# Four one-bank PSUM tiles, a pair-wise plain eviction and a split attention copy in a linear-attention and two-FFN kernel

## The chip, the cores and the metric

The kernel runs on one core of one Trainium2 chip. The metric is the device time of one execution in microseconds (us), as the median of several runs. Engines are named as the profile names them: PE (TensorE matmul), PEld (its weight load), DVE (VectorE), ACT (ScalarE), POOL (GpSimd) and SP (SyncE, which issues all DMAs here).

## The reference

Everything is in fp32. Linear attention over 8 batches, 8 heads, 576 positions and head width 64 feeds an RMS norm over the head width; the result, seen as 4608 tokens of 512 channels, goes through two feed-forward networks of width 2048.

```python
kv = np.einsum('bhsd,bhse->bhde', k, v)
out = np.einsum('bhsd,bhde->bhse', q, kv)
rms = np.sqrt(np.mean(out * out, axis=-1, keepdims=True) + 1e-06)
x = (out / rms * g_norm).transpose(0, 2, 1, 3).reshape(B * S, H * D)
h = x @ w_in;  g = np.maximum(h, 0) + alpha * np.minimum(h, 0);  x = g @ w_out      # layer 0
h = x @ w_in2; g = h / (1 + np.exp(-1.702 * h));                 y = g @ w_out2     # layer 1
```

## The kernel before

**Blocks and the two ways of multiplying.** The 4608 tokens are nine blocks j of 512. An fp32 product is made of three fp32r matmuls of 128x512 (high by high, high by low, low by high). Blocks 0, 1 and 2 of layer 0 and block 0 of layer 1 are done in plain form (`gemm_in` into a bank named h, `gemm_out` into four banks named y, one for each chunk c of 128 rows, summed over 16 steps m). All other blocks are done two at a time by a seven-product scheme (`pair_in`, `pair_out`): a step is one product, six matmuls. In-steps go into banks named X or Z, out-steps into two-bank tiles named V or W. The in-steps of two values of k (call them k0 and k1) alternate: product p for k0, product p for k1, next product for k0, and so on. X holds products 1, 6, 7, 4 on top of each other, Z product 2, and then 5 and 3; after each product the bank is read (ACT, L1166, 128x512 copy; DVE, L1158 and L1156, 128x512 add) before the next product is added in it. A run's out-steps start 26 in-steps after its in-steps (`LAGP`); from there in-steps and out-steps alternate.

**Where the order comes from.** The program first notes its operations with an engine, a cost and what each reads and writes. `arrange` plays them through a small model of the engines and gives each a start and a place in memory. `emit` does that `PASSES` times with other weights (random numbers from `SEED`), keeps the pass with the earliest end and writes all operations out in the order of their starts. So every engine's queue is fixed before the run; the tile framework puts in the semaphore waits, from the order in which instructions are written out and from the tiles that they touch.

**PSUM.** Eight banks of 512 words per partition. `SLOTS` cuts them in four slots of two banks: one of class h (plain h, Z, the first block's transposed x), two of class y (the plain y, V, W), one of class a (kv sums, transposed q, attention output ops, later blocks' transposed x, X). `at_place` opens one framework tile for a whole slot and hands out slices of it, as long as any part of the slot is in use:

```python
SLOTS += [(UNITS + 2 * i, 2, c) for i, c in enumerate("hyya")]
...
        opened[s] = (stay, kind, pool.tile([P, size * UNIT], kind, tag=f"s{s}", name=name))
    _, kind, t = opened[s]
    t = t[:, (u - u0) * UNIT : (u - u0 + n) * UNIT]
```

Thus a slot's two banks carry one tile name: a transposed q can appear as "kvps", the first plain h as "xTps".

**Attention (`job_out`).** For later blocks the output of two pairs of heads takes both a banks at once ("aa"), and one ACT copy of 128x1024 (L608) moves it to SBUF. **Weights.** In the first 200 us the 16 weight tiles of layer 0 are unpacked on ACT, DVE and POOL and split by DVE into their low part (L698 and L700, tile w). **The end of a plain block.** Each of the four chunks y is copied by an instruction of its own, even chunks on ACT and odd ones on DVE, and stored by one DMA.

Of the kernel before, what the change touches and what calls it, by code (L numbers as in the profile page):

```python
# [10 lines left out]
F32 = mybir.dt.float32  # L11
# [4 lines left out]
AF = mybir.ActivationFunctionType  # L16
# [3 lines left out]
P = 128  # L20
TB = 512
# [28 lines left out]
MM, TR, ACT, DVE, POOL, ISSUE, LAND, RATE, HOP = 0.227, 0.109, 0.63, 0.67, 1.27, 0.55, 2.2, 0.335, 0.2  # L50
ACT2, DVE2, POOL2 = 1.06, 1.17, 2.35
# [8 lines left out]
BACKLOG = 2.0  # L60
URGENT = 10.0
LD_LOW = {"4": 10}
PASSES = 30
SEED = 1
GAP, SLOW = 1.8, 3.4

RINGS = (3, 2, 2, 6)
# [11 lines left out]
def linear_attention_two_ffn_kernel(  # L79
# [25 lines left out]
    nc = tc.nc  # L105
# [43 lines left out]
    ops = []  # L149
# [57 lines left out]
    def tl(key):  # L207
        return tiles[key]
# [346 lines left out]
    def job_out(j, pp):  # L555

        heads = (2 * pp, 2 * pp + 1)
        bank, sq, xn = ((what, j, pp) for what in ("ops", "sq", "xn"))
        small = {}
        parts = [(t, *run) for t in range(NT4) for run in runs((NT4 * j + t) * P, P)]  # L560
        batches = sorted({b for _, _, _, b, _ in parts})

        def fn():
            for t, off, n, b, s in parts:
                for i, p in enumerate(heads):
                    nc.tensor.matmul(
                        tl(bank)[off : off + n, i, t],
                        lhsT=tl(("qT", j, p))[:, t * P + off : t * P + off + n],
                        rhs=tl(("kvb", b % 2))[:, p, :],
                        start=True,  # L570
                        stop=True,
                    )

        held = ("oc", j, pp) if j else bank

        def o3(key=held):
            t = tl(key)
            return t if key == ("oc", j, pp) else t.rearrange("p i t (e d) -> p (i t e) d", d=D)
# [22 lines left out]
        note(  # L601
            "PE", 0.46 * len(parts), fn,
            reads=[x for p in heads for x in ((("qT", j, p), 0), held_by["qT", j, p])] + [(("kvb", b % 2), p) for b in batches for p in heads],
            writes=[(bank, 0)], new=[(bank, [P, 2, NT4, P], F32, "aa" if j else "yy")], aside=True,
        )
        if j:
# [4 lines left out]
        note(  # L611
            "ACT", ACT2, lambda: nc.scalar.activation(out=tl(sq), in_=o3(), func=AF.Square), reads=[(held, 0)],
            writes=[(sq, 0)], new=[(sq, [P, 2 * G, D], F32, "4")],
        )
        note("DVE", 1.4, mean, reads=[(sq, 0)], writes=[(("sa", j, pp), 0)])
        note("ACT", 0.21, root, reads=[(("sa", j, pp), 0)], writes=[(("sr", j, pp), 0)])
        note(
            "DVE", 1.9, scale, reads=[(held, 0), (("sr", j, pp), 0), (("sa", j, pp), 0)], writes=[(xn, 0)],
            new=[(xn, [P, 2 * G, D], F32, "4")],
        )  # L620

# [342 lines left out]
    def gemm_out(l, j, m, m0, m1):  # L964

        if l == 0:
            weight1("wo", m)
        else:
            weight2("wo", m)
        (w, w_keys), gs = w_key(l, "wo", m), ("gs", l, j, m)  # L970
        for c in range(4):
            y = ("y", l, j, m0, c)
            sl = slice(c * P, (c + 1) * P)

            def fn(y=y, sl=sl, c=c):
                gh, gl = tl(gs)[:, 0], tl(gs)[:, 1]
                if l == 0:
                    wt = w()[:, c // 2, :, c % 2 * P : (c % 2 + 1) * P]
                    trip = ((wt[:, 0], gh), (wt[:, 0], gl), (wt[:, 1], gh))
                else:  # L980
                    wh, wl = w()[:, :, 0], w()[:, :, 1]
                    trip = ((gh[:, sl], wh), (gh[:, sl], wl), (gl[:, sl], wh))
                mm3(tl(y), trip, m == m0, m == m1)

            note(
                "PE", 3 * MM, fn, reads=[*w_keys, (gs, 0), (gs, 1)], writes=[(y, 0)],
                new=[(y, [P, TB], F32, "y")] if m == m0 else [],
            )
        if m < m1:
            return  # L990
        for c in range(4):
            y, ev, part = ("y", l, j, m0, c), ("ev", l, j, m0, c), ("part", l, j, c)
            new = [(ev, [P, TB], F32, "2")]
            if m0 > 0:
                note(
                    "SP", ISSUE, lambda part=part, c=c: nc.sync.dma_start(out=tl(part), in_=yp[c]),
                    reads=[(("yp", c), 0)], writes=[(part, 0)], new=[(part, [P, TB], F32, "2")], ahead=20.0,
                    slack=None, mb=0.26,
                )
                note(  # L1000
                    "DVE", DVE,
                    lambda y=y, ev=ev, part=part: nc.vector.tensor_tensor(
                        out=tl(ev), in0=tl(y), in1=tl(part), op=ALU.add
                    ),
                    reads=[(y, 0), (part, 0)], writes=[(ev, 0)], new=new, slack=2.0,
                )
            else:
                copy = nc.vector.tensor_copy if c % 2 else nc.scalar.copy

                def evict(y=y, ev=ev, copy=copy):  # L1010
                    if l == 0:
                        copy(tl(ev), tl(y))
                        return
                    for h in range(2):
                        sl = slice(h * HB, (h + 1) * HB)
                        copy(
                            tl(ev)[:, sl].rearrange("p (i c f) -> p i c f", c=2, f=32),
                            tl(y)[:, sl].rearrange("p (c i f) -> p i c f", c=2, f=32),
                        )

                note(
                    "DVE" if c % 2 else "ACT", DVE if c % 2 else ACT, evict, reads=[(y, 0)], writes=[(ev, 0)], new=new,
                    slack=2.0,
                )
            if l:
                dst, key = out[j * TB + c * P : j * TB + (c + 1) * P, :], ("out", j, c)
            elif m == M - 1:
                dst, key = x2d[j][c], ("dr", 1, j, c)
            else:
                dst, key = yp[c], ("yp", c)  # L1030
            note(
                "SP", ISSUE, lambda dst=dst, ev=ev: nc.sync.dma_start(out=dst, in_=tl(ev)), reads=[(ev, 0)],
                writes=[(key, 0)], mb=0.26,
            )

    def plain(steps, jobs):
# [342 lines left out]
```

## Time and profile before

| | |
|---|---|
| median of 3 runs | 1572.46 us (1572.04 to 1574.06) |
| the profiled execution | 1569.55 us, its span 1567.8 us |
| PE busy | 1520.3 us, 97% of the span, 7376 matmuls |
| DVE busy | 1150.9 us, 73% |
| ACT busy | 764.7 us, 49% |
| POOL busy | 279.6 us, 18% |
| mean granted TensorE clock | 0.994 of full speed |

The span runs from the first to the last instruction; 1.75 us of the execution lie around it. Matmuls are pipelined, and one of 128x512 shows some 390 ns though the next starts after about 227, so busy time hides short gaps: the count of matmuls in a stretch says more.

### The profile page before, as it was taken

The numbers are of one execution on the slowest core, as the hardware profiler recorded it, in microseconds if no ns is written. First come the engines' busy times: TensorE is split into PE (matmuls) and PEld (weight loads), VectorE is DVE, ScalarE is ACT, GpSimd is POOL, SyncE is SP. The second block draws the span as 40 slices with busy tenths as digits, with TensorE's granted clock in tenths as the row PEclk, the third lists the DMA queues.
The fourth block names the chain that finished last, engine by engine and source line by source line (L and its number), as shares of the span: only waits on it lengthen the run. The fifth ranks groups of instructions, "written<-read, shape, count | busy, mean of one in ns | idle before, by whom it ended". The sixth has DMA issues, their size and how long they took to land.

```text
span 1567.8 us, 19613 instructions
## 1 busy us (share of the span) xinstructions
PE 1520.3 (97%) x7376; PEld 1244.5 (79%) x7376; DVE 1150.9 (73%) x1170; ACT 764.7 (49%) x958; POOL 279.6 (18%) x186
## 2 busy tenths in 40 slices
PE   5899999999899999999999999999999999999998
PEld 4688888887687878877877888888888888888787
DVE  4999965698689998999998867664766485557511
ACT  4876544455355455544455655434544454445221
POOL 1322531275322123212420320000000000000000
PEclk8999999999999999999999999999999999999999
DMA  9899786757689789979798997576667676755963
GB/s 263 253 311 292 197 213 191 200 167 272 219 285 341 256 310 334 322 253 355 259 331 310 351 321 284 186 233 220 242 196 229 198 253 206 227 195 189 280 189 107
DMA packets 240654, 393.48 MB, mean 251 GB/s; under 512 B 94128, under 2 KB 124848, under 8 KB 240560
## 3 DMA queue, kind: packets, MB, share of 16 engines
q1 hardware_dynamic: 240560, 392.23, 77.2%
q8 instruction: 58, 0.95, 0.2%
q14 instruction: 36, 0.29, 0.1%
HBM read 302.00 MB, written 90.18 MB: 250 GB/s over the span
## 4 chain that ended last, share of the span: by engine, by line
PE 66%; DVE 2%; ACT 1%; issue 1%; DMA 0%; POOL 0%; SPq 0%; DVEq 0%; ACTq 0%; POOLq 0%
PE V L927 18%; PE X L927 17%; PE Z L927 13%; PE W L927 13%; PE h L927 3%; PE y L927 3%; ACT gr L691 0%; DVE gr L698 0%; DMA t<-x2d 0%; DVE gl L1158 0%; ACT gl L1166 0%; DVE gt L1158 0%; POOL kvb L774 0%; ACT xc L691 0%; DVE gt L891 0%
## 5 line engine op out<-in xcount | busy, mean ns | idle before, releaser
L927 PE MATMUL X<-xc,pi 128*128 128x512 f32 x912 | 233.7, 392 | 4.2 <-DVE gl L1158 3.3
L927 PEld LDWEIGHTS X<-xc,pi 128*128 128x128 f32 x912 | 169.6, 188 | 45.5 <-DVE gl L1158 7.6
L927 PE MATMUL V<-gr,x 128*128 128x512 f32 x804 | 203.9, 389 | 0.0
L927 PEld LDWEIGHTS V<-gr,x 128*128 128x128 f32 x804 | 151.0, 188 | 31.7
L927 PE MATMUL Z<-xc,pi 128*128 128x512 f32 x648 | 166.7, 393 | 2.9 <-ACT gl L1166 2.8
L927 PE MATMUL W<-gr,x 128*128 128x512 f32 x636 | 161.3, 389 | 0.0
L927 PEld LDWEIGHTS Z<-xc,pi 128*128 128x128 f32 x648 | 120.3, 188 | 33.5 <-ACT gl L1166 7.1
L927 PE MATMUL h<-x,w 128*128 128x512 f32 x576 | 142.6, 395 | 0.7 <-ACT acc L952 0.7
L927 PEld LDWEIGHTS W<-gr,x 128*128 128x128 f32 x636 | 119.4, 188 | 24.9
L927 PEld LDWEIGHTS h<-x,w 128*128 128x128 f32 x576 | 106.2, 188 | 22.6 <-ACT acc L952 1.1
L691 ACT ACTIVATE gr<-gt 128x1024 fp32r<-128x1024 f32 x84 | 88.8, 1059 | 63.1 <-DVE gt L891 24.8
L698 DVE TENSOR_TENSOR gr<-gl,gr 128x1024 fp32r<-128x1024 f32 x56 | 74.9, 1338 | 56.9 <-ACT gr L691 56.9
L927 PE MATMUL V<-gr,po 128*128 128x512 f32 x456 | 114.6, 389 | 0.0
L698 DVE TENSOR_TENSOR gr<-gt,gr 128x1024 fp32r<-128x1024 f32 x84 | 105.2, 1257 | 3.7 <-ACT gr L691 3.7
L927 PEld LDWEIGHTS V<-gr,po 128*128 128x128 f32 x456 | 85.6, 188 | 17.8
L927 PE MATMUL X<-xc,po 128*128 128x512 f32 x360 | 91.5, 389 | 1.3 <-ACT gl L1181 1.3
L858 POOL TENSOR_TENSOR da<-da 128x256 f32<-128x256 f32 x68 | 71.2, 1048 | 82.5 <-DVE wsp L698 77.9
L927 PEld LDWEIGHTS X<-xc,po 128*128 128x128 f32 x360 | 67.5, 188 | 15.6 <-ACT gl L1181 1.7
L927 PE MATMUL W<-gr,po 128*128 128x512 f32 x312 | 78.4, 389 | 0.0
L927 PE MATMUL Z<-xc,po 128*128 128x512 f32 x300 | 77.0, 392 | 0.2
L1166 ACT ACTIVATE gt<-X 128x512 f32<-128x512 f32 x64 | 38.3, 598 | 79.1 <-PE X L927 79.0
L691 ACT ACTIVATE gr<-gl 128x1024 fp32r<-128x1024 f32 x56 | 59.3, 1058 | 33.2 <-PE V L927 22.0
(507 smaller groups left out, 2698.7 us busy)
## 6 DMA issues: line engine op xcount, KB each, us to landing
po<-w1wo SPq DMA_DIRECT2D x69, 512.0 KB, 3.8
pi<-w0wi SPq DMA_DIRECT2D x68, 512.0 KB, 5.7
x<-w0wo SPq DMA_DIRECT2D x68, 512.0 KB, 5.2
pi<-w1wi SPq DMA_DIRECT2D x62, 512.0 KB, 5.0
po<-w1wi SPq DMA_DIRECT2D x57, 512.0 KB, 4.7
x<-w1wo SPq DMA_DIRECT2D x52, 512.0 KB, 3.9
raw<-in_moe_w_in_dram SPq DMA_DIRECT2D x16, 1024.0 KB, 6.7
raw<-in_moe_w_out_dram SPq DMA_DIRECT2D x16, 1024.0 KB, 8.0
```

Source lines behind the costliest of these rows:

```text
L691: "ACT", ACT2 if both else ACT, lambda: nc.scalar.activation(out=part(0), in_=value(), func=AF.Copy, scale=1.0 if scale is None else scale),
L698: nc.vector.tensor_tensor(out=part(1), in0=value(), in1=high, op=ALU.subtract)
L858: lambda o=o, a=a, b=b, op=op: nc.gpsimd.tensor_tensor(out=quarter(o), in0=quarter(a), in1=quarter(b), op=op),
L927: nc.tensor.matmul(o, lhsT=x, rhs=y, start=start and n == 0, stop=stop and n == 2, skip_group_check=True)
L1166: nc.scalar.activation(out=val(), in_=tl(bank), func=func, scale=sign)
```

## The change

The slot of class h and the slot of class a are each cut in two slots of one bank; the two y slots become places for two-bank tiles only (`yy`). So every X, Z, h, qTps, xTps, kvps and ops is a tile of its own bank. The four plain chunks y become two tiles of two chunks; layer 0 copies (or adds) and stores a tile of two chunks by one instruction and one DMA each; layer 1 still copies chunk by chunk, but each copy waits for both chunks of its tile. The attention of later blocks is made, and copied out, by one pair of heads at a time: two PE notes and two ACT copies of 128x512 where there was one of 128x1024. The plan is searched in 12 passes from seed 14 in place of 30 from seed 1.

```diff
-PASSES = 30
-SEED = 1
+PASSES = 12
+SEED = 14
...
-SLOTS += [(UNITS + 2 * i, 2, c) for i, c in enumerate("hyya")]
-SIZE = {"8": 4, "4": 2, "2": 1, "h": 1, "y": 1, "a": 1, "hh": 2, "yy": 2, "aa": 2}
-HOME = {c: [s for s, x in enumerate(SLOTS) if x[2] == (c[0] if c[0] in "hya" else "sb")] for c in SIZE}
+SLOTS += [(UNITS + i, 1, c) for i, c in enumerate("hhaa")] + [(UNITS + 4 + 2 * i, 2, "yy") for i in range(2)]
+SIZE = {"8": 4, "4": 2, "2": 1, "h": 1, "a": 1, "yy": 2}
+HOME = {c: [s for s, x in enumerate(SLOTS) if x[2] == (c if c[0] in "hya" else "sb")] for c in SIZE}
...
-        def fn():
+        def fn(hs):
             for t, off, n, b, s in parts:
-                for i, p in enumerate(heads):
+                for i in hs:
                     nc.tensor.matmul(
-                        tl(bank)[off : off + n, i, t],
-                        lhsT=tl(("qT", j, p))[:, t * P + off : t * P + off + n],
-                        rhs=tl(("kvb", b % 2))[:, p, :],
+                        (tl(("ops", j, heads[i])) if j else tl(bank)[:, i])[off : off + n, t],
+                        lhsT=tl(("qT", j, heads[i]))[:, t * P + off : t * P + off + n],
+                        rhs=tl(("kvb", b % 2))[:, heads[i], :],
                         start=True,
                         stop=True,
...
+        for hs in ((0,), (1,)) if j else ((0, 1),):
+            own = [heads[i] for i in hs]
+            to = ("ops", j, own[0]) if j else bank
             note(
-                "ACT", ACT2, lambda: nc.scalar.copy(tl(held), o3(bank)), reads=[(bank, 0)], writes=[(held, 0)],
-                new=[(held, [P, 2 * G, D], F32, "4")],
-            )
-        note(
-            "ACT", ACT2, lambda: nc.scalar.activation(out=tl(sq), in_=o3(), func=AF.Square), reads=[(held, 0)],
+                "PE", 0.23 * len(hs) * len(parts), lambda hs=hs: fn(hs),
+                reads=[x for p in own for x in ((("qT", j, p), 0), held_by["qT", j, p])] + [(("kvb", b % 2), p) for b in batches for p in own],
+                writes=[(to, 0)], new=[(to, [P, NT4, P], F32, "a") if j else (to, [P, 2, NT4, P], F32, "yy")], aside=True,
+            )
+            if j:
+                note(
+                    "ACT", ACT,
+                    lambda to=to, i=hs[0]: nc.scalar.copy(
+                        tl(held)[:, i * G : (i + 1) * G], tl(to).rearrange("p t (e d) -> p (t e) d", d=D)
+                    ),
+                    reads=[(to, 0)] + [(held, 0)] * hs[0], writes=[(held, hs[0])],
+                    new=[(held, [P, 2 * G, D], F32, "4")] if hs[0] == 0 else [],
...
+                "PE", 3 * MM, fn, reads=[*w_keys, (gs, 0), (gs, 1)], writes=[(y, c % 2)],
+                new=[(y, [P, 2, TB], F32, "yy")] if m == m0 and c % 2 == 0 else [],
             )
         if m < m1:
             return
-        for c in range(4):
-            y, ev, part = ("y", l, j, m0, c), ("ev", l, j, m0, c), ("part", l, j, c)
-            new = [(ev, [P, TB], F32, "2")]
+        for h in range(2):
...
+            y, part = ("y", l, j, m0, h), ("part", l, j, h)
+            both = [(y, 0), (y, 1)]
+            if l:
+                for i in range(2):
+                    ev, copy = ("ev", l, j, m0, h, i), nc.vector.tensor_copy if i else nc.scalar.copy
+
+                    def evict(y=y, ev=ev, copy=copy, i=i):
+                        for x in range(2):
+                            sl = slice(x * HB, (x + 1) * HB)
+                            copy(
+                                tl(ev)[:, sl].rearrange("p (n c f) -> p n c f", c=2, f=32),
+                                tl(y)[:, i, sl].rearrange("p (c n f) -> p n c f", c=2, f=32),
+                            )
+
+                    note(
+                        "DVE" if i else "ACT", 0.8, evict, reads=both, writes=[(ev, 0)], new=[(ev, [P, TB], F32, "2")],
+                        slack=2.0,
...
+                copy = nc.vector.tensor_copy if h else nc.scalar.copy
                 note(
-                    "DVE" if c % 2 else "ACT", DVE if c % 2 else ACT, evict, reads=[(y, 0)], writes=[(ev, 0)], new=new,
-                    slack=2.0,
-                )
-            if l:
-                dst, key = out[j * TB + c * P : j * TB + (c + 1) * P, :], ("out", j, c)
-            elif m == M - 1:
-                dst, key = x2d[j][c], ("dr", 1, j, c)
+                    "DVE" if h else "ACT", DVE2 if h else ACT2, lambda y=y, ev=ev, copy=copy: copy(tl(ev), tl(y)),
+                    reads=both, writes=[(ev, 0)], new=new, slack=2.0,
```

**PE, first in-steps of the first pair (blocks 3 and 4), while no out-step runs yet.** A number behind a name tells tiles apart; x12 is two steps, k0 and k1. Before:

```order
L927 MATMUL X_3213<-xc_3020,x_695 128x512 x12
L927 MATMUL Z_3232<-xc_3081,gs_3102 128x512 x12
L927 MATMUL X_3213<-xc_3108,x_296 128x512 x12
L927 MATMUL Z_3271<-xc_3092,x_695 128x512 x12
L927 MATMUL Z_3271<-xc_3114,gs_3139 128x512 x12
```

Now:

```order
L934 MATMUL X_3266<-xc_3062,x_2237 128x512 x6
L934 MATMUL X_3277<-xc_3062,x_2237 128x512 x6
L934 MATMUL Z_3289<-xc_3106,gs_3167 128x512 x6
L934 MATMUL Z_3298<-xc_3106,gs_3167 128x512 x6
L934 MATMUL X_3266<-xc_3191,gs_430 128x512 x6
L934 MATMUL X_3277<-xc_3191,gs_430 128x512 x6
L934 MATMUL Z_3326<-xc_3181,gs_430 128x512 x6
L934 MATMUL Z_3335<-xc_3181,gs_430 128x512 x6
L934 MATMUL Z_3326<-xc_3146,gs_3167 128x512 x6
L934 MATMUL Z_3335<-xc_3146,gs_3167 128x512 x6
```

The order of the steps is the same. What moved is the tile: where k0 and k1 shared X_3213 and Z_3271, each has a tile of its own, so the row of twelve is two of six.

**ACT, the copies out of these banks.** gt and gl are the SBUF tiles copied to. Before:

```order
L1166 ACTIVATE gt_3229<-X_3213,sign_sb_71 128x512 x4
L691 ACTIVATE wsp_3281<-da_1932 128x4x256
L1166 ACTIVATE gl_3291<-Z_3271,sign_sb_71 128x512 x2
L691 ACTIVATE wsp_3340<-xt_2004 128x4x256
L1166 ACTIVATE gl_3291<-X_3213,sign_sb_71 128x512 x2
```

Now:

```order
L1189 ACTIVATE gt_3285<-X_3266,sign_sb_71 128x512
L1189 ACTIVATE gt_3285<-X_3277,sign_sb_71 128x512
L1189 ACTIVATE gt_3285<-X_3266,sign_sb_71 128x512
L1189 ACTIVATE gt_3285<-X_3277,sign_sb_71 128x512
L1189 ACTIVATE gl_3343<-Z_3326,sign_sb_71 128x512
L1189 ACTIVATE gl_3343<-Z_3335,sign_sb_71 128x512
L698 ACTIVATE wsp_3357<-kvb_118 128x4x256
L1189 ACTIVATE gl_3343<-X_3266,sign_sb_71 128x512
```

The copies from X and Z keep their order among themselves, and each now names its own bank's tile. A weight split (wsp) that stood ahead of the two copies from Z now stands behind them.

**PE, the start of the program: attention of block 0.** kvps is the sum over k and v, qTps a transposed q, ops the output of two pairs of heads. Before:

```order
L475 MATMUL kvps_137<-ldkv_125 64x64 x8
L475 MATMUL kvps_137<-kR_115 64x64 x2
L543 MATMUL kvps_137<-ident_69,ldkv_125 128x128 x8
L475 MATMUL kvps_137<-ldkv_132 64x64 x8
L475 MATMUL kvps_137<-kR_115 64x64 x2
L566 MATMUL ops_198<-kvb_118,ldkv_125 128x128 x8
L475 MATMUL kvps_137<-ldkv_132 64x64 x8
L475 MATMUL kvps_137<-kR_115 64x64 x2
L543 MATMUL qTps_243<-ident_69,kvb_118 128x128 x8
L566 MATMUL ops_269<-kvb_118 128x128 x8
```

Now:

```order
L475 MATMUL kvps_137<-ldkv_125 64x64 x8
L475 MATMUL kvps_137<-kR_115 64x64 x2
L543 MATMUL qTps_169<-ident_69,ldkv_125 128x128 x4
L543 MATMUL qTps_179<-ident_69,ldkv_125 128x128 x4
L475 MATMUL kvps_137<-ldkv_132 64x64 x8
L475 MATMUL kvps_137<-kR_115 64x64 x2
L566 MATMUL ops_200<-kvb_118,ldkv_125 128x128 x8
L475 MATMUL kvps_137<-ldkv_132 64x64 x8
L475 MATMUL kvps_137<-kR_115 64x64 x2
L543 MATMUL qTps_228<-ident_69,ldq_148 128x128 x4
L543 MATMUL qTps_241<-ident_69,ldq_148 128x128 x4
L566 MATMUL ops_262<-kvb_118,ldq_148 128x128 x8
```

The transposes of q have tiles of their own and no longer stand in the tile of the kv sums; the last two come from a fresh buffer (ldq) where they waited for kvb to be free; both outputs ops come before any transpose of x, as before.

## Rows read from the trace of the kernel before

**Rows 1.** The page: busy times; a group with its busy, mean ns and idle before.

```profile
PE 1520.3 (97%) x7376; PEld 1244.5 (79%) x7376; DVE 1150.9 (73%) x1170; ACT 764.7 (49%) x958; POOL 279.6 (18%) x186
...
L927 PE MATMUL V<-gr,x 128*128 128x512 f32 x804 | 203.9, 389 | 0.0
```

**Rows 2.** Windows: from:to length, busy of each engine (count), PEclk, DMA share, GB/s.

```profile
21.00:60.48 39.48, 25.65 (x189) 20.40 (x185) 37.55 (x48) 27.67 (x37) 12.55 (x5) 0.78 0.92 283
60.48:200.00 139.52, 138.98 (x917) 116.28 (x916) 134.15 (x156) 92.51 (x127) 50.13 (x25) 1.00 0.92 261
200.00:377.69 177.69, 176.99 (x1088) 147.32 (x1087) 129.30 (x164) 84.94 (x122) 63.74 (x49) 1.00 0.69 198
377.69:430.45 52.76, 43.93 (x182) 32.94 (x180) 31.97 (x29) 18.48 (x24) 25.61 (x20) 1.00 0.73 256
430.45:880.00 449.55, 442.69 (x1920) 357.91 (x1919) 416.33 (x381) 232.19 (x263) 107.85 (x66) 1.00 0.87 305
880.00:1440.00 560.00, 559.85 (x2461) 460.72 (x2460) 360.42 (x350) 273.20 (x330) 17.09 (x14) 1.00 0.71 235
...
1473.17:1483.29 10.12, 8.75 (x38) 6.61 (x36) 3.85 (x4) 2.46 (x4) 0.00 (x0) 1.00 1.07 284
```

**Rows 3.** Timeline, first in-steps: start, length, what [idle before <-who ended it].

```profile
377.69 2.88 PE L927 MATMUL X<-xc,x 128*128 128x512 f32 x12
...
380.61 1.27 ACT L1166 ACTIVATE gt<-X,sign_sb 128x512 f32<-128x512 f32 x2 [2.13 <-PE X L927]
...
387.33 1.06 ACT L691 ACTIVATE wsp<-da 128x1024 fp32r<-128x1024 f32 x1
...
389.51 1.66 PE L927 MATMUL Z<-xc,gs 128*128 128x512 f32 x6 [0.78 <-ACT gl L1166]
...
391.21 0.69 ACT L1166 ACTIVATE gl<-Z,sign_sb 128x512 f32<-128x512 f32 x1 [1.75 <-PE Z L927]
...
391.95 1.64 PE L927 MATMUL Z<-xc,gs 128*128 128x512 f32 x6 [0.78 <-ACT gl L1166]
```

**Rows 4.** Timeline, in-steps and out-steps alternating.

```profile
529.44 1.52 PE L927 MATMUL Z<-xc,pi 128*128 128x512 f32 x6
...
532.38 1.66 PE L927 MATMUL Z<-xc,pi 128*128 128x512 f32 x6
```

**Rows 5.** Timeline, first plain steps of the last block.

```profile
1475.89 0.84 PE L927 MATMUL h<-po,w 128*128 128x512 f32 x3
...
1476.77 0.60 ACT L952 ACTIVATE acc<-h 128x512 f32<-128x512 f32 x1 [17.76 <-PE h L927]
...
1477.41 1.66 PE L927 MATMUL h<-x,w 128*128 128x512 f32 x6 [0.69 <-ACT acc L952]
```

**Rows 6.** Timeline, the start of the program.

```profile
14.87 1.12 PE L475 MATMUL kvps<-ldkv 128*64 128x64 f32 x16 [0.68 <-ACT ldkv L551]
...
21.07 1.22 DVE L582 TENSOR_REDUCE sa<-ldkv 128x16 f32<-128x1024 f32 x1 [20.20 <-ACT ldkv L612]
...
48.74 2.93 PE L927 MATMUL xTps<-x,w 128*128 128x512 f32 x6 [5.09 <-DVE x L664]
...
60.48 1.63 PE L927 MATMUL y<-gs,w 128*128 128x512 f32 x6
```

**Rows 7.** Timeline, the last of the 16 weight splits of layer 0.

```profile
68.82 1.22 DVE L698 TENSOR_TENSOR w<-kvb,w 128x1024 fp32r<-128x1024 f32 x1
...
195.70 3.37 DVE L698 TENSOR_TENSOR w<-xn,w 128x1024 fp32r<-128x1024 f32 x1
...
200.49 2.88 PE L927 MATMUL y<-x,w 128*128 128x512 f32 x12
```

**Rows 8.** Timeline, copies out of PSUM: attention, plain block, out-step, the end.

```profile
55.71 0.59 ACT L551 COPY ldkv<-qTps 128x512 f32<-128x512 f32 x1 [0.18 <-PE qTps L543]
...
60.81 1.02 ACT L608 COPY ldkv<-ops 128x1024 f32<-128x1024 f32 x1 [0.32 <-PE ops L566]
...
1563.05 0.76 DVE L1016 COPY ev<-y 128x256 f32<-128x256 f32 x2 [0.61 <-ACT ev L1016]
```

More of the change, by code (lines that the diff above doesn't have):

```diff
@@ L574, in job_out, with o3 @@
         held = ("oc", j, pp) if j else bank
-        def o3(key=held):
-            t = tl(key)
-            return t if key == ("oc", j, pp) else t.rearrange("p i t (e d) -> p (i t e) d", d=D)
+        def o3():
+            return tl(held) if j else tl(held).rearrange("p i t (e d) -> p (i t e) d", d=D)
         def mean():
@@ L599, in scale @@
             nc.vector.tensor_tensor(out=tl(xn), in0=o3(), in1=r.to_broadcast([P, 2 * G, D]), op=ALU.mult)
-        note(
-            "PE", 0.46 * len(parts), fn,
-            reads=[x for p in heads for x in ((("qT", j, p), 0), held_by["qT", j, p])] + [(("kvb", b % 2), p) for b in batches for p in heads],
-            writes=[(bank, 0)], new=[(bank, [P, 2, NT4, P], F32, "aa" if j else "yy")], aside=True,
-        )
-        if j:
-            note(
-                "ACT", ACT2, lambda: nc.scalar.copy(tl(held), o3(bank)), reads=[(bank, 0)], writes=[(held, 0)],
-                new=[(held, [P, 2 * G, D], F32, "4")],
-            )
-        note(
-            "ACT", ACT2, lambda: nc.scalar.activation(out=tl(sq), in_=o3(), func=AF.Square), reads=[(held, 0)],
+        for hs in ((0,), (1,)) if j else ((0, 1),):
[15 more added lines that the diff above has]
+                )
+        oc = [(held, 0), (held, 1)] if j else [(held, 0)]
+        note(
+            "ACT", ACT2, lambda: nc.scalar.activation(out=tl(sq), in_=o3(), func=AF.Square), reads=oc,
             writes=[(sq, 0)], new=[(sq, [P, 2 * G, D], F32, "4")],
@@ L617, in job_out @@
         note(
-            "DVE", 1.9, scale, reads=[(held, 0), (("sr", j, pp), 0), (("sa", j, pp), 0)], writes=[(xn, 0)],
+            "DVE", 1.9, scale, reads=[*oc, (("sr", j, pp), 0), (("sa", j, pp), 0)], writes=[(xn, 0)],
             new=[(xn, [P, 2 * G, D], F32, "4")],
@@ L982, in fn @@
                     trip = ((gh[:, sl], wh), (gh[:, sl], wl), (gl[:, sl], wh))
-                mm3(tl(y), trip, m == m0, m == m1)
+                mm3(tl(y)[:, c % 2], trip, m == m0, m == m1)
             note(
-                "PE", 3 * MM, fn, reads=[*w_keys, (gs, 0), (gs, 1)], writes=[(y, 0)],
-                new=[(y, [P, TB], F32, "y")] if m == m0 else [],
+                "PE", 3 * MM, fn, reads=[*w_keys, (gs, 0), (gs, 1)], writes=[(y, c % 2)],
+                new=[(y, [P, 2, TB], F32, "yy")] if m == m0 and c % 2 == 0 else [],
             )
@@ L1004, in gemm_out @@
                     ),
-                    reads=[(y, 0), (part, 0)], writes=[(ev, 0)], new=new, slack=2.0,
+                    reads=[*both, (part, 0)], writes=[(ev, 0)], new=new, slack=2.0,
                 )
             else:
[L1008 to L1019, printed above, removed]
+                copy = nc.vector.tensor_copy if h else nc.scalar.copy
                 note(
-                    "DVE" if c % 2 else "ACT", DVE if c % 2 else ACT, evict, reads=[(y, 0)], writes=[(ev, 0)], new=new,
-                    slack=2.0,
-                )
-            if l:
-                dst, key = out[j * TB + c * P : j * TB + (c + 1) * P, :], ("out", j, c)
-            elif m == M - 1:
-                dst, key = x2d[j][c], ("dr", 1, j, c)
+                    "DVE" if h else "ACT", DVE2 if h else ACT2, lambda y=y, ev=ev, copy=copy: copy(tl(ev), tl(y)),
+                    reads=both, writes=[(ev, 0)], new=new, slack=2.0,
+                )
+            if m == M - 1:
+                dst, keys = x2d[j], [(("dr", 1, j, 2 * h + i), 0) for i in range(2)]
             else:
-                dst, key = yp[c], ("yp", c)
+                dst, keys = yp, [(("yp", h), 0)]
             note(
-                "SP", ISSUE, lambda dst=dst, ev=ev: nc.sync.dma_start(out=dst, in_=tl(ev)), reads=[(ev, 0)],
-                writes=[(key, 0)], mb=0.26,
+                "SP", ISSUE,
+                lambda dst=dst, ev=ev, h=h: nc.sync.dma_start(
+                    out=dst[2 * h : 2 * h + 2].rearrange("c p f -> p c f"), in_=tl(ev)
+                ),
+                reads=[(ev, 0)], writes=keys, mb=0.52,
             )
```

24 lines of the change are left out of this document (19 added, 5 removed).

## Prediction

> **What bounds the kernel now.** I began with the busy times of the page: PE is busy 97% of the span and no other engine over 73% [rows 1]. So the kernel can only become faster where PE loses time. To find where, I took the windows view and counted matmuls, since a busy PE hides short gaps. The reader should first see 880 to 1440: 2461 matmuls in 560.00 us, PE busy 559.85, granted clock 1.00 [rows 2]. That is 0.2276 us for one, 1.365 us for a step of six, and it is the pace of a PE that never waits. Against it:
>
> - 377.69 to 430.45, the first in-steps of the first pair (26 of them without an out-step, then two of each kind): 30 steps, 180 matmuls, should take 40.97 us and take 52.76. Lost: 11.8.
> - 430.45 to 880, in-steps and out-steps alternating in layer 0: 1920 matmuls should take 437.0 us and take 449.55. Lost: 12.6, of which only 449.55 - 442.69 = 6.9 shows as idle. The rest sits in slow restarts: after a wait six matmuls show 1.66 us, otherwise 1.52 [rows 3, 4].
> - 1473.17 to 1483.29, the first plain steps of the last block: 36 matmuls should take 8.2 us and take 10.12. Lost: 1.9.
> - From 60.48 to 377.69 PE idles only 0.54 + 0.70 us; in 21 to 60.48 it idles 13.83 of 39.48, at a mean granted clock of 0.78 of full speed, between the two levels of 1.2 and 2.4 GHz [rows 2].
>
> Then I read the timeline for what PE waits for. PE does both steps of product 1 into X from 377.69 to about 380.57. The copy of k0's bank could start when the first six end, near 379.1, but ACT sits idle 2.13 us and starts at 380.61, when k1's six have ended [rows 3]. With Z it goes on: PE waits 0.78 us at 389.51 for ACT; then ACT idles 1.75 us until PE's six have ended, and starts the next copy at 391.21; then PE waits 0.78 again, at 391.95 [rows 3]. ACT and PE take turns on two different banks. The plain steps show the same: the copy of the first h starts at 1476.77, not when its own matmuls end (before 1475.89) but after three matmuls for the other h, and PE's rest of that h waits until 1477.41 for the copy [rows 5]. In the order both halves carry one tile name. My reading: the waits are set for the tile, so a bank waits for its neighbour.
>
> **The change part by part.**
>
> *Own tiles for X, Z, h and a.* Between two uses of one bank lie k1's six (1.365 us) in the first stretch. The copy takes 0.69 [rows 3], so 0.67 us are to spare where ACT comes at once. But ACT also has instructions of 1.06 in its queue (the split at 387.33 [rows 3]), and a copy behind one of these is up to 1.06 - 0.67 = 0.4 late, plus the slow restart of 0.14. The tight places are product 5 to 3, 7 to 4, and 4 to the next 1: six in 14 steps, about eleven in 26. If every second one still loses 0.54 us, 3 of 11.8 stay. I take a gain of 8.5; bounds 4 (every tight place still loses 0.7) and 11.8.
>
> In the alternating stretch a bank's next use comes at the earliest three steps later (out, k1, out): 4.1 us, minus 0.7 for the copy leaves 3.4 to spare. Before, k1's step had to wait for k0's copy with one out-step between: 1.365 - 0.7 = 0.67 to spare. Most delays of DVE and ACT here are one instruction of 1.06 to 1.3, and the longest split is 3.37 [rows 7], just within 3.4. DVE stays busy 416.33 of 449.55 us [rows 2], so a chain of late instructions can still reach PE. I take 10 of the 12.6; bounds 5 and 12.6. In the plain steps at the end the copy of the first h no longer touches PE: 1.8, at least 1.2.
>
> The Trainium skill bears on this (PSUM — Partial Sum Buffer, section "PSUM bank collisions raise a hardware error"): accesses are to be guarded by bank and quadrant, and different banks may be used at once. By it alone every one of these waits is needless, which would be the whole 26.3 us (an estimate from that page and the rows); the rows agree as far as they show the waits on another bank's work, and I keep less because the engines' queues also bind.
>
> *The start.* PE's transposes of q no longer stand in the tile of the kv sums. Before, kv work at 14.87 waited 0.68 us for a copy of a transposed q [rows 6], and two such copies lay in that chain, so DVE's first reduction (21.07) can come 1 to 3 us earlier. The first y stands at 60.48 after a wait of 5.09 us for the last split of x at 48.74 [rows 6]. The new plan puts the transposes of x together, ahead of all h, so y can be much earlier, perhaps 10 us. But I doubt that this lasts. From 21 to 200 us DVE is busy 37.55 + 134.15 = 171.7 of 179 us [rows 2], and its last weight split of layer 0 ends at 195.70 + 3.37 = 199.07, just 1.4 us before the y step at 200.49 that stands behind it [rows 7]. PE can't pass that point until DVE has done the same 16 splits. What is left is DVE's earlier start, 1 to 3 us, the 1.4 us, and part of DVE's 7.3 idle us. I take 3; bounds -4 (another order, with more splits stretched as that one of 3.37) and +10.
>
> *Attention by one pair of heads.* Two copies of 128x512 at 0.58 to 0.59 replace one at 1.02 [rows 8]: 0.15 us more of ACT, 16 times, 2.4 us. ACT is busy 49% [rows 1], and PE's attention work needs one free bank instead of two at once. Zero; if ACT's slack were gone there, 2.4.
>
> *Plain eviction by two chunks.* One 128x1024 copy (about 1.0 us, as the 1.02 above) for two of 0.59: nothing on PE's path, because the y banks are next needed by out-steps, 26 in-steps of 1.365, or 35 us, after the plain stretch of layer 0 ends. If that cover were gone, the wait for the second chunk would cost one half step, 0.7 us, at three evictions. At the very end both chunks still share one tile, so DVE's last copy will still stand behind ACT's (1563.05 [rows 8]). Zero.
>
> *Passes and seed.* Another plan of the same work. The step order in the pairs is the same in the rows of the order; I count nothing and let it widen the range.
>
> Sum: 8.5 + 10 + 1.8 + 3 = 23.3. From the profiled execution, 1569.55 - 23.3 = 1546.3. The runs' median, 1572.46, stands 2.9 above that execution, so in its terms 1549.
>
> **The rivals.** A difference of 0.2%, 3.1 us, is about what a measurement of this kernel can tell from no change.
>
> *It is a shortage of banks, not the shared tile.* PE would wait at 389.51 because there are two Z banks and both are in use, and the change gives no more banks. Then only the start gains: 1572.5 - 3 = 1569.5. Against it: ACT's 2.13 and 1.75 us idle [rows 3] are waits of a reader that had its data, and a shortage of banks doesn't make a reader wait. The Trainium skill holds this rival (Perfetto Trace Analysis, section "Optimization Strategy": consistent bubbles can mean too little PSUM for the next tile). Chance 0.10.
>
> *DVE sets the pace from 430 to 880.* With 92.6% of its time taken, a PE that runs ahead soon waits for DVE's adds and low parts instead: 4 of 12.6 come back, 5 of 11.8, 1.8 and 2: 1572.5 - 12.8 = 1559.7. For it: that busy share. Against it: V steps, which take DVE's low parts, show an idle time of 0.0 ahead of 804 matmuls [rows 1], and PE gains only 2% on DVE. Chance 0.15.
>
> *The early start lasts.* The first y comes some 10 us earlier and DVE's work is so ordered that the last split keeps up: 10 in place of 3, 1542. Chance 0.14.
>
> *Slower: DVE's splits collide with POOL in the first 200 us.* Most low-part splits take 1.22 us and that at 195.70 takes 3.37 [rows 7], while POOL is at work. If the new order made all 16 so long, PE would wait 16 x 2.15 = 34 us at the last y, and the sum would be 1572.5 - 20.3 + 34 = 1586. It decides from about eleven such splits on (23.3 / 2.15). Against it: POOL does the same number of adds, and the order of splits on DVE is alike. Chance 0.06.
>
> **How the numbers follow.** My forecast has 0.55, with 1543 to 1556 of its own. The range reaches up to the DVE rival and most of the bank rival, and down to most of the early start: 1540 to 1566. Outside are the slower rival (0.06), about 0.08 of the bank rival, and some 0.05 below. Faster by over 0.2%: 0.55 + 0.15 + 0.14 + half of the bank rival = 0.89. Within 0.2%: the other half, 0.05. Slower: 0.06.
>
> **What will show it.** Right, if in the first in-steps ACT starts k0's copy about 0.2 us after k0's six and not after k1's; if the first 30 steps take 41.5 to 46 us where they took 52.76; if the alternating stretch in layer 0 runs at 0.228 to 0.229 us a matmul (before, 449.55 / 1920 = 0.234); if the first h of the last block are not held by each other's copy. The first y should come near 50 to 55 us, and the y step behind the last split near 197. Wrong, if PE still waits on X and Z for 0.8 us with ACT idle ahead of it, or if V and W steps begin to wait for DVE's low parts, or if the last split of layer 0 comes after 200 us.

## The result and the profile after

The changed kernel takes 1536.11 us (median of 4 runs, 1534.85 to 1536.82) against 1572.25 (4 runs, 1570.04 to 1574.06): ratio 0.977, 95% interval 0.9753 to 0.9787. Faster, as forecast, but 12.9 us below the 1549 and 3.9 below the range.

The page of the kernel after answers to [rows 1]. Among its groups, Z's first has 0.4 us of idle time.

```profile
PE 1505.9 (98%) x7376; PEld 1245.1 (81%) x7376; DVE 1150.7 (75%) x1165; ACT 767.0 (50%) x971; POOL 286.5 (19%) x186
...
L934 PE MATMUL Z<-xc,pi 128*128 128x512 f32 x564 | 143.2, 389 | 0.4 <-DVE gt L1181 0.4
```

PE's busy time fell by 14.4 us and the rest of its span from 47.5 to 28.1. The busy time fell because part of each wait counts as busy: a matmul shows 0.39 us though the next can start after 0.227, and the restart behind a wait is slow. The windows of after, cut where those of [rows 2] were cut: the start, 30 steps, the next 1920 matmuls, the rest up to the last block, the last block's first 36 matmuls, and at the end 80 us of the alternating steps:

```profile
0.00:374.30 374.30, 351.87 (x2288) 290.48 (x2289) 305.75 (x363) 213.05 (x311) 146.60 (x97) 0.99 0.82 239
374.30:415.43 41.13, 41.09 (x182) 33.70 (x180) 34.10 (x37) 19.77 (x25) 19.13 (x12) 1.00 0.99 347
415.43:851.37 435.94, 435.49 (x1922) 360.28 (x1921) 419.81 (x383) 234.92 (x265) 111.42 (x68) 1.00 0.90 316
851.37:1441.61 590.24, 590.24 (x2606) 488.74 (x2605) 375.97 (x363) 278.30 (x335) 9.34 (x11) 1.00 0.71 230
1441.61:1449.77 8.16, 8.16 (x38) 6.76 (x37) 3.85 (x4) 2.46 (x4) 0.00 (x0) 1.00 1.08 289
640.00:720.00 80.00, 80.00 (x355) 66.24 (x354) 79.46 (x74) 38.91 (x46) 15.95 (x10) 1.00 0.88 307
```

From the first in-step to the last block the waits of PE sum up to those 0.4 us, and the last row has DVE busy 79.46 of 80.00 us beside a PE that runs on.

Between the two profiled executions lie 33.7 us: the start 377.69 - 374.30 = 3.4; the 30 steps 52.76 - 41.13 = 11.6; the 1920 matmuls 449.55 - 435.94 = 13.6; the rest (880 to 1473.17 before, 593.17) 2.9; the last block, from its first matmul to its last, 89.16 before and 87.20 after, 2.0; the tail behind it 0.2. The tail differs from kernel to kernel (4.55 to 5.44 us over all fourteen; e9, which ends as after does, has 4.73), so its 0.2 can't be put down to the change.

The first in-steps in the timeline of after (columns as in [rows 3]):

```profile
374.30 2.88 PE L934 MATMUL X<-xc,x 128*128 128x512 f32 x12
...
375.86 0.69 ACT L1189 ACTIVATE gt<-X,sign_sb 128x512 f32<-128x512 f32 x1 [0.74 <-PE X L934]
...
377.22 0.69 ACT L1189 ACTIVATE gt<-X,sign_sb 128x512 f32<-128x512 f32 x1 [0.67 <-PE X L934]
...
382.69 5.38 PE L934 MATMUL Z<-xc,gs 128*128 128x512 f32 x23
384.02 0.69 ACT L1189 ACTIVATE gl<-Z,sign_sb 128x512 f32<-128x512 f32 x1 [0.67 <-PE Z L934]
385.38 0.69 ACT L1189 ACTIVATE gl<-Z,sign_sb 128x512 f32<-128x512 f32 x1 [0.67 <-PE Z L934]
...
385.97 1.05 ACT L698 ACTIVATE wsp<-kvb 128x1024 fp32r<-128x1024 f32 x1
```

The first copy from X starts 1.56 us after PE's first matmul, that is 0.2 us after the first six (1.365), where it started 2.92 after it before. Twenty-three matmuls into Z then stand in one row without a gap, while ACT empties one bank and PE fills the other. The split that could have made a copy late (385.97) stands behind both copies.

The start, in the timeline, answers to [rows 6, 7]:

```profile
18.16 1.22 DVE L581 TENSOR_REDUCE sa<-ldkv 128x16 f32<-128x1024 f32 x1 [17.29 <-ACT ldkv L619]
...
47.21 0.49 PE L934 MATMUL y<-gs,w 128*128 128x512 f32 x1 [0.75 <-ACT gs L698]
...
188.15 1.18 DVE L705 TENSOR_TENSOR w<-oc,w 128x1024 fp32r<-128x1024 f32 x1
...
193.91 2.88 PE L934 MATMUL y<-gs,w 128*128 128x512 f32 x12
```

DVE's first reduction comes 2.9 us earlier, the first y 13.3, the end of the last weight split 9.7; at the first in-step 3.4 of it are left.

### The profile page after: what moved, and what is told of

It is laid out like the page before. It is cut to its first block, busy times and chain, and to the rows that moved or that the text cites. A ratio compares the mean times of both kernels' runs of the same rounds, so it can differ in the third digit from the quotient of the medians.

```text
span 1534.0 us, 19665 instructions
## 1 busy us (share of the span) xinstructions
PE 1505.9 (98%) x7376; PEld 1245.1 (81%) x7376; DVE 1150.7 (75%) x1165; ACT 767.0 (50%) x971; POOL 286.5 (19%) x186
## 4 chain that ended last, share of the span: by engine, by line
PE 78%; DVE 2%; DMA 1%; issue 0%; ACT 0%; SPq 0%; DVEq 0%; ACTq 0%
PE X L934 20%; PE V L934 20%; PE W L934 15%; PE Z L934 15%; PE y L934 4%; PE h L934 4%; DMA raw<-in_moe_w_out_dram 1%; PE ops L566 0%; DMA po<-w0wo 0%; DVE wsp L705 0%; DVE dr__1325 L598 0%; DVE sa L592 0%; PE qTps L543 0%; DVE x L705 0%; DVE dr__1325 L637 0%
## 5 line engine op out<-in xcount | busy, mean ns | idle before, releaser
L934 PE MATMUL V<-gr,po 128*128 128x512 f32 x1032 | 260.2, 389 | 0.0
L934 PEld LDWEIGHTS V<-gr,po 128*128 128x128 f32 x1032 | 193.7, 188 | 40.2
L934 PE MATMUL X<-xc,pi 128*128 128x512 f32 x804 | 203.7, 389 | 0.0
L934 PE MATMUL W<-gr,po 128*128 128x512 f32 x756 | 190.7, 389 | 0.0
L934 PEld LDWEIGHTS W<-gr,po 128*128 128x128 f32 x756 | 141.9, 188 | 29.5
L934 PE MATMUL y<-gs,w 128*128 128x512 f32 x492 | 121.0, 394 | 1.7 <-DVE gs L705 0.9
L934 PE MATMUL X<-xc,po 128*128 128x512 f32 x468 | 118.7, 389 | 0.0
L934 PEld LDWEIGHTS y<-gs,w 128*128 128x128 f32 x492 | 90.8, 188 | 20.8 <-DVE gs L705 1.2
L934 PEld LDWEIGHTS Z<-xc,po 128*128 128x128 f32 x372 | 69.8, 188 | 14.5
L1179 DVE TENSOR_TENSOR gt<-Z,gt 128x512 f32<-128x512 f32 x64 | 44.1, 689 | 34.1 <-PE Z L934 33.6
```

The costliest lines, as they stand in the source:

```text
L934: nc.tensor.matmul(o, lhsT=x, rhs=y, start=start and n == 0, stop=stop and n == 2, skip_group_check=True)
L1179: nc.vector.tensor_tensor(out=val(), in0=tl(bank), in1=val(), op=ALU.add)
```

## The experiments

Twelve kernels ran, each with 4 runs, beside 7 of the kernel before on the same chip (medians of before there: 1570.7 to 1571.89). Their stages, from windows of each trace: first in-step; the 26 in-steps until the first out-step; alternating until the last block; the last block.

| kernel | median us | ratio to before (95%) | first in-step | in-steps alone | alternating | last block |
|---|---|---|---|---|---|---|
| before | 1572.25 | | 377.69 | 45.39 | 1050.08 | 89.16 |
| after | 1536.11 | 0.977 (0.9753 to 0.9787) | 374.30 | 35.69 | 1031.62 | 87.20 |
| e1, h and a shared | 1578.00 | 1.0049 (1.0034 to 1.0063) | 384.54 | 44.44 | 1055.08 | 89.16 |
| e5, h shared | 1554.78 | 0.989 (0.9873 to 0.9906) | 378.43 | 41.55 | 1039.34 | 89.16 |
| e6, a shared | 1559.53 | 0.9925 (0.991 to 0.9939) | 382.20 | 39.61 | 1044.18 | 87.20 |
| e4, before with h cut | 1551.97 | 0.9884 (0.9869 to 0.9899) | 374.53 | 40.53 | 1041.91 | 87.20 |
| e2, after, 30 passes seed 1 | 1539.41 | 0.9801 (0.9787 to 0.9816) | 377.40 | 35.36 | 1033.12 | 87.20 |
| e3, before, 12 passes seed 14 | 1594.14 | 1.0147 (1.013 to 1.0164) | 383.57 | 48.75 | 1069.50 | 89.16 |
| e7, single chunks, 12 / 14 | 1550.61 | 0.9868 (0.9854 to 0.9883) | 388.89 | 35.84 | 1033.76 | 87.20 |
| e9, after's order, chunks one by one | 1535.78 | 0.9777 (0.9762 to 0.9791) | 375.32 | 35.69 | 1031.62 | 87.20 |
| e10, single chunks, 30 / 1 | 1538.19 | 0.9793 (0.9778 to 0.9807) | 377.28 | 35.39 | 1031.31 | 87.20 |
| e11, single chunks, 12 / 2 | 1538.79 | 0.9798 (0.9783 to 0.9812) | 375.03 | 35.39 | 1034.06 | 87.20 |
| e12, after, 12 / 2 | 1541.95 | 0.9819 (0.9802 to 0.9835) | 378.58 | 35.44 | 1032.91 | 87.20 |
| e8, last chunks apart | 1536.59 | 0.9779 (0.9764 to 0.9793) | 375.55 | 35.69 | 1031.62 | 87.20 |

The kernels ran on different chips, and the medians of before lie 1.6 us apart; a difference of 1 or 2 us between two medians is no finding.

My theory was that the gain is the tiles': a wait belongs to a tile and not to a bank. The rivals were the order that the new search found, the plain eviction, and a shortage of banks.

**e1: the tiles alone undone.** In `at_place`, banks of classes h and a become slices of one two-bank tile each; every engine's order is that of after.

```diff
+        if where in 'ha':
+            if where not in opened:
+                opened[where] = ps.tile([P, 2 * UNIT], F32, tag=f"g{where}", name=name)
+            u0 = min(x[0] for x in SLOTS if x[2] == where)
+            t = opened[where][:, (u - u0) * UNIT : (u - u0 + n) * UNIT]
```

> The changed kernel with its instructions in the same order on every engine; only the two h banks are again slices of one tile, and the two a banks of another. If the waits come from the shared tile, the losses of before come back: the first 30 pair steps near 51 us (after about 41), the alternating stretch near 0.233 us a matmul, and 1536 + 30 = about 1566 us in all (1556 to 1576). If the new plan (passes, seed) made the gain, it stays at 1535 to 1539.

1578.00 us: 41.9 more than after, 2 above the range that I gave. By stages of the profiled executions: 10.2 in the start, 8.8 in the in-steps alone, 23.5 in the alternating stretch, 2.0 in the last block. The longest waits of e1's PE from the first in-step to the last block, in us, times and longest (X and Z now go by their tile's first names, kvps and xTps):

```profile
PE xTps L943 <- ACT gl L1198: 5.5, 8, 0.8
PE kvps L943 <- ACT gl L1198: 5.2, 10, 1.6
PE kvps L943 <- DVE gl L1190: 4.4, 6, 1.9
...
```

And its first in-steps:

```profile
384.54 2.88 PE L943 MATMUL kvps<-xc,x 128*128 128x512 f32 x12
...
387.46 1.27 ACT L1198 ACTIVATE gt<-kvps,sign_sb 128x512 f32<-128x512 f32 x2 [2.11 <-PE kvps L943]
```

ACT again starts 2.92 us after PE's first matmul, with both copies in one row, as in [rows 3]. The same banks in the same order lose the gain and more, so neither a shortage of banks nor the order made it. That e1 is even slower than before (6.9 us in the start, 5.0 in the alternating stretch) may come from its tiles, which stay open for the whole program, or from its order, which was found for banks that don't share; the two were not separated.

**e5 and e6: one class at a time.** The edit is that of e1 with `where in 'h'` and `where in 'a'`.

> The kernel after, with the two banks of class h (plain h, Z, the first block's transposed x) again slices of one tile; every engine's order is that of after, X and the rest of class a keep tiles of their own. Theory (a wait belongs to a tile, and each class pays for its own sharing): of the 42 us that sharing both classes cost, this takes some 20: the first in-steps 4 to 5 us longer than in after, the alternating stretch 8 to 14 longer, the last block 2.0 longer, waits of PE on Z and h but none on X; 1550 to 1562 us. And this run and the one with only class a shared add up to 42 (35 to 50). Rival (one late bank holds back both classes, so either alone costs nearly all): 1566 to 1578 us.

> The kernel after, with the two banks of class a (X, kv sums, transposed q, attention output, later blocks' transposed x) again slices of one tile; every engine's order is that of after, Z and h keep tiles of their own. Theory: the first in-steps about 5 us longer than in after and the alternating stretch about 10 longer (as in the kernel before with only class h cut, where class a was still shared), the last block as in after, the start 0 to 8 longer (kv sums and transposed q share again); 1551 to 1560 us, waits of PE on X and none on Z. Rival (either alone costs nearly all): 1566 to 1578 us.

18.7 and 23.4 us over after, together 42.1 where e1 lost 41.9: the losses add, and the rival falls. The waits of PE behind the first in-step, first e5, then e6:

```profile
PE xTps L943 <- ACT gl L1198: 5.2, 7, 0.8
PE xTps L943 <- ACT acc L968: 1.4, 2, 0.7
...
PE X L943 <- DVE gl L1190: 1.0, 2, 0.8
...
```

```profile
PE kvps L943 <- ACT gl L1198: 5.2, 10, 1.6
PE kvps L943 <- DVE gl L1188: 1.9, 2, 1.0
...
```

With h shared PE waits on Z (and on the last block's h, which costs its 1.96 us); with a shared it waits on X, longest 1.6. Small misses: e5 still has 1.0 us of waits on X, where I expected none, and loses 5.9 us in the in-steps alone (4 to 5 expected) and 7.7 in the alternating stretch (8 to 14); e6 loses 3.9 and 12.6 there (5 and 10).

**e4: half of the change done.** In the kernel before only the h slot is cut in two.

```diff
-SLOTS += [(UNITS + 2 * i, 2, c) for i, c in enumerate("hyya")]
+SLOTS += [(UNITS + i, 1, "h") for i in range(2)] + [(UNITS + 2 + 2 * i, 2, c) for i, c in enumerate("yya")]
```

> The kernel before with only the h slot cut in two tiles (Z and plain h), class a still one tile, search of before. By the shared tile theory about half of the 30 us comes back, that of Z and h: 1553 to 1563 us, with no PE wait on Z or h left and those on X as before. If only the change as a whole, or the search, counts: 1568 to 1576 us.

1551.97 us, a little below what I expected. One line of `SLOTS` brings half of the gain: of the 19 us, 3.2 lie in the start, where the search also found another order, and 4.9, 8.2 and 2.0 in the three stages behind it. What e4's PE still waits for behind the first in-step:

```profile
PE X L927 <- DVE gl L1158: 3.8, 7, 0.9
PE X L927 <- ACT gl L1166: 2.4, 4, 0.8
...
PE Z L927 <- ACT gl L1166: 0.3, 1, 0.3
```

X, in the slot that is still shared, and hardly Z.

**e2 and e3: the search exchanged.** after with the old passes and seed, before with the new ones.

```diff
-PASSES = 12
-SEED = 14
+PASSES = 30
+SEED = 1
```

> The changed kernel, planned with 30 passes from seed 1 as before. If the tiles made the gain, 1533 to 1542 us, with the pair stretches as after the change and only the first 375 us different. If the new search made it, 1555 to 1570 us.

> The kernel before, planned with 12 passes from seed 14. If the tiles made the gain, this one stays at 1567 to 1578 us with PE waits on X and Z as before. If the new search made it, it falls to 1536 to 1550 us.

e2 is 3.3 us over after. In the profiled executions its start is 3.1 longer; the alternating stretch, where I expected no difference, is 1.5 longer. e3 is 23 us over before and 16 over what I had expected. Its waits behind the first in-step:

```profile
PE X L927 <- DVE gl L1158: 9.6, 7, 3.4
PE Z L927 <- ACT gl L1166: 6.0, 7, 1.6
...
PE V L927 <- DVE gr L698: 1.9, 2, 1.1
```

The longest wait on X grew from 1.5 us in before to 3.4. So with shared tiles the order was worth 23 us between two searches, and with tiles of their own 3 to 6 (e2, e12) where the form is that of after. Two searches of before are few to call that a law.

**e7: the plain eviction undone.** Layer 0's chunks are copied, added and stored one by one (their two-bank tiles stay); the search then finds another order.

```diff
-            ev = ("ev", l, j, m0, h)
-            new = [(ev, [P, 2, TB], F32, "4")]
+            for i in range(2):
+                c = 2 * h + i
+                ev, part = ("ev", l, j, m0, c), ("part", l, j, c)
+                new = [(ev, [P, TB], F32, "2")]
...
-                    reads=both, writes=[(ev, 0)], new=new, slack=2.0,
+                        reads=[(y, i)], writes=[(ev, 0)], new=new, slack=2.0,
```

> The kernel after, with layer 0's plain output copied, added and stored chunk by chunk again (its two-bank y tiles stay); the search of the order finds another order at the start. Theory (the form of the plain eviction is off PE's path): every stage from the first in-step on as in after within 1 us, the start within 4 us of after's 374.3; 1533 to 1541 us. Rival (the fewer instructions and DMAs free engine time that the start needs): the start 5 us or more longer, 1541 to 1548 us.

14.5 us over after, beyond even the rival's range. In the profiled executions its start is 14.6 longer, and the alternating stretch 2.1, where I had allowed 1. In e7's timeline, and in its windows of the same places:

```profile
384.03 5.06 PE L934 MATMUL y<-gs,w 128*128 128x512 f32 x11 [4.92 <-DVE gs L705]
```

```profile
378.61:384.03 5.42, 0.50 (x1) 0.18 (x1) 5.42 (x4) 0.00 (x0) 5.18 (x4) 0.84 0.32 97
384.03:388.89 4.86, 4.86 (x11) 3.80 (x12) 3.99 (x3) 0.59 (x1) 4.62 (x5) 0.50 0.47 180
```

Just before the first in-step PE waits 4.92 us for DVE's low part, DVE being busy all of that time, and then runs 11 matmuls at a granted clock of 0.50. Was this the form, or the order? Four runs to tell:

**e9 to e12.** e9 keeps after's order and puts two instructions of one chunk where one of two chunks stood, for copies, adds and DMAs; e10 and e11 are e7 with other searches; e12 is after with another search.

```diff
-                    lambda y=y, ev=ev, copy=copy: copy(tl(ev), tl(y)),
+                    lambda y=y, ev=ev, copy=copy: [copy(tl(ev)[:, i], tl(y)[:, i]) for i in range(2)],
```

> The kernel after with every engine's order kept, but wherever layer 0's plain output is copied, added, stored or read back by one instruction of two chunks, two instructions of one chunk stand in its place. Theory (the run with single chunks lost 14.5 us to the order that its search found, above all a 4.9 us wait of PE for DVE's low part just before the first in-step and the lower granted clock behind it): 1534 to 1539 us, first in-step at 374 to 377 us. Rival (two chunks by one instruction and one DMA is itself worth it): 1542 to 1551 us, first in-step at 380 to 389.

> The kernel after with layer 0's plain output copied, added and stored chunk by chunk, as in the run with single chunks, but the order searched in 30 passes from seed 1 in place of 12 from seed 14. Theory (the order, not the form): the start differs from that run's 388.89 and comes back to within 8 us of after's 374.3 (371 to 382), 1533 to 1544 us. Rival (the form): the start stays at 384 to 394, 1546 to 1556 us.

> As the run before it, with 12 passes from seed 2. Theory (the order): a third start, anywhere from 371 to 392 us, and at least one of the two single-chunk runs with other seeds below 382; all stages behind the first in-step as in after within 2 us. Rival (the form): 384 to 394 in both.

> The kernel after with 12 passes from seed 2 in place of seed 14, nothing else changed. Theory (the order of the start is worth several us either way): the first in-step at 371 to 390 us, behind it every stage as in after within 2 us (in-steps 35.7, alternating 1031.6, last block 87.2). Rival (with two-chunk eviction the start doesn't depend on the order): the first in-step within 2 us of 374.3 to 377.4, as with 12 passes from seed 14 and 30 from seed 1.

e9 takes 1535.78, within the intervals equal to after; e10 and e11 1538.19 and 1538.79. So the form of the plain eviction is worth nothing that these runs can tell, and e7's loss was its order's. With the same passes and seed, single chunks are no slower than two-chunk eviction in e10 against e2 (1539.41) and in e11 against e12 (1541.95). e12, with after's form, starts 4.3 us later than after and is 5.8 us slower. In e11 the alternating stretch is 2.4 longer than in after, a little over the 2 that I allowed. None of these beats after by more than its measurement tells.

**e8: the tail.** The last block's chunks 2 and 3 get a one-bank tile each.

```diff
-            y = ("y", l, j, m0, c // 2)
+            apart = l == 1 and c > 1
+            y = ("y", l, j, m0, c) if apart else ("y", l, j, m0, c // 2)
...
+                    if h:
+                        y = ("y", l, j, m0, 2 + i)
+                        both = [(y, 0)]
```

> The kernel after, with the last block's chunks 2 and 3 in two one-bank tiles of class a, which are free there, in place of one two-bank tile; nothing else is changed. Theory (ACT and DVE, which copy one chunk each out of the last tile, take turns because they name one tile): the last two copies run at once, and from the last matmul to the end it takes 0.6 to 0.8 us less than after's 5.22; the whole is 1535.4, too little for the runs' intervals to tell from 1536.1. Rival (the two engines take turns for another reason, or the store of the last chunk sets the end anyway): the copies follow each other as before and the tail stays at 5.0 to 5.4.

The tail takes 5.23 us, as in after (5.22), as the rival has it; but the copies did what the theory says. First after, then e8:

```profile
1525.92 2.88 PE L934 MATMUL y<-gs,po 128*128 128x512 f32 x12
...
1528.84 0.65 ACT L1008 COPY ev<-y 128x256 f32<-128x256 f32 x2 [0.71 <-PE y L934]
...
1529.52 0.76 DVE L1008 COPY ev<-y 128x256 f32<-128x256 f32 x2 [0.60 <-ACT ev L1008]
```

```profile
1527.19 2.88 PE L934 MATMUL y<-gs,po 128*128 128x512 f32 x12
...
1529.42 0.65 ACT L1012 COPY ev<-y 128x256 f32<-128x256 f32 x2
1529.43 0.76 DVE L1012 COPY kvb<-y 128x256 f32<-128x256 f32 x2 [5.49 <-ACT kvb L1012]
1530.11 0.76 DVE L1012 COPY ev<-y 128x256 f32<-128x256 f32 x2
```

In after PE's last matmul ends at 1528.80 and DVE's copy of the last chunk starts 0.72 us behind it, when ACT's copy has ended. In e8 PE ends at 1530.07 and the same copy starts 0.04 us behind it, waiting for no copy of ACT's; only DVE's copy of chunk 1 still waits for ACT's of chunk 0, and these two still share a PSUM tile. So a tile for each reader ended the turn taking here too, and the last copy ended 0.7 us sooner after PE. The end didn't move with it. What both kernels have alike is the stores: in the 3.00 us that begin about 0.25 us behind the last matmul, after first, then e8:

```profile
1529.05:1532.05 3.00, 0.00 (x0) 0.00 (x0) 0.76 (x2) 0.44 (x2) 0.00 (x0) 0.95 0.91 343
1530.31:1533.31 3.00, 0.00 (x0) 0.00 (x0) 0.55 (x2) 0.00 (x0) 0.00 (x0) 1.00 0.91 343
```

The DMA engines are busy at a share of 0.91 and move 343 GB/s in both. So it is likely that the stores of the last four chunks set the end, as the second half of the rival says; no run moved the stores to show it.

Undoing the attention copy alone wasn't tried: one instruction for two pairs of heads needs the two-bank tile that the rest of the change removes.

## Why the prediction was right in kind and too small

The mechanism was the one forecast: e1 shows the tiles to be the cause, e4 gets half of the gain from one cut slot in the code of before, and the signs of it came: the copy 0.2 us after k0's six, h no longer held, no waits of 0.8 us on X and Z. The sizes went past what I had set as signs: the first 30 steps 41.13 us (41.5 to 46), the 1920 matmuls 0.2271 us each (0.228 to 0.229), the first y at 47.21 (50 to 55), the y behind the last split at 193.91 (near 197). The bank rival falls with the 0.4 us that PE now waits on Z with as many banks. The Trainium skill (PSUM — Partial Sum Buffer, section "PSUM bank collisions raise a hardware error") has only a bank and its quadrants to guard; the estimate that I drew from it, 26.3 us for the three places, stood nearer to the 27.2 measured (11.6 + 13.6 + 2.0) than my own 20.3.

The forecast is 12.9 us too high. The step that failed is the sizing of the two large terms, "I take a gain of 8.5" and "I take 10 of the 12.6":

- **The part kept for late readers** (3.3 in the first stretch, 2.6 in the second) hardly existed. I had every second tight place lose 0.54 us, and argued that "a chain of late instructions can still reach PE" since DVE is busy 93%. In after it happens once in each stretch:

```profile
387.90 5.93 PE L934 MATMUL X<-xc,gs 128*128 128x512 f32 x24
...
463.64 1.65 PE L934 MATMUL Z<-xc,pi 128*128 128x512 f32 x6 [0.45 <-DVE gt L1181]
```

  The 24 matmuls of the first row show 0.3 us more than 24 without a wait (5.60). The second row lost 0.7 with its slow restart. In the 80 us with DVE busy for 79.46, PE waits for nothing. Nor was it luck of the order that puts the split behind the two copies: in e12 a split stands ahead of the two copies from Z, and the 26 in-steps take 35.44 us against 35.69 in after; in the other orders with tiles of their own they take 35.36 to 35.84. Measured: 11.6 for 8.5.
- **The benchmark pace** of 0.2276 us was itself taken from a stretch with waits, which the trace of before shows as slow restarts (PE, 880 to 1440):

```profile
925.38 1.65 PE L927 MATMUL Z<-xc,po 128*128 128x512 f32 x6
```

  Fifteen matmuls start there more than 0.3 us after the one ahead of them; behind 851.37 in after none does. After runs 2606 matmuls in 590.24, or 0.2265, and e1 needs 593.47 for the same stretch. At that pace the 1920 matmuls lost 14.7, not 12.6, and the stretch behind 880, for which I had counted nothing, gave 2.9. Measured 13.6 and 2.9, for 10 and 0 (the cuts of before and after differ by two matmuls there, so 0.45 of the 2.9 belongs to the 13.6). "PE busy 559.85 of 560.00" hid short waits in the slow restarts, the very thing that I had named for 430 to 880.
- **The start** was 3 and came at 3.4, and that it fits is luck. I had counted the tiles and left out the order: with the new tiles other searches start the in-steps at 377.40 (e2) and 378.58 (e12), where before has 377.69, and in after's own order shared tiles cost the start 10.2 us (e1). That PE's early start doesn't last was right, though the place that I named wasn't its limit: the last split ended 9.7 us earlier. From 320 to the first in-step DVE is busy 53.75 of 54.30 us (56.31 of 57.69 before), and in e7 it is DVE that PE waits for at the end of this stretch. That DVE sets the end of the start in after too is likely, but no run moved DVE's work there to show it. I had put that rival in 430 to 880.
- **The rest**: last block 2.0 for 1.8; tail 0.2 for 0, within what it differs by anyway. Plain eviction nothing (e9). Passes and seed, counted as nothing, brought 3.3 with the new tiles (e2), 3.1 of it within the start's term. The attention copy shows in no wait, but was not separated.
- **The step from the profile to the median**: I added 2.9 us, as for before; after's profiled execution, 1535.81, is only 0.3 below its median. That is 2.6 of the 12.9. The terms' shortfall is 3.1 + 3.6 + 2.9 + 0.4 + 0.2 + 0.2 = 10.4.

The slower rival (DVE's splits colliding with POOL) didn't come: first in-step 3.4 us earlier, last split 1.18 us long. But 5 of the 16 splits of layer 0 are stretched in after (1.76 to 3.43 us), 3 in before (1.76 to 3.42): its condition came nearer, and eleven were needed.

## What to carry to other kernels

If two engines take turns on two different banks, look at which tile each instruction names: give every bank that has a reader of its own a tile of its own before anything else is tuned, and try it by the one line that cuts the slot. Take the pace of a free engine from a stretch in which nothing waits at all, or from the shortest repeated step: 0.5% of error over the alternating steps hid 5.0 us of losses here (14.7 - 12.6 = 2.1, and 2.9). And when an order comes out of a search, compare the changed code in the old order (as e9) or over several searches before judging a part of it: one search made a part worth nothing look like 14.5 us.

## What the runs showed of the hardware

- A wait of PE can cost more than its length. In e7 the granted clock was 0.84 over the stretch of the wait, and 4.92 us without work were followed by 4.86 us at a granted clock of 0.50, the lower level of 1.2 GHz, in which 11 matmuls ran at 0.44 us each; at 0.2265 they would have taken 2.5. The waits of 0.8 us on X and Z in before left the clock at 1.00 [rows 2].
- DVE at 99% and PE at 100% of 80 us, at the full granted clock, went side by side in after without a wait of PE (640 to 720).
- The stores of the last four chunks took as long in e8 as in after, though the last copy was done 0.7 us sooner: 343 GB/s over 3.00 us, at a DMA share of 0.91, in both.
